# Gate steps, layer norm by blocks and rate rows in the prologue of an S4-convolution and SwiGLU training step

## The chip, the cores and the metric

One Trainium2 chip, one of its cores. The metric is the device time of one execution in microseconds (us). The kernel computes a forward pass and all gradients, in one launch.

## The reference, cut to what matters

```python
xn = layernorm(x)                          # x: 2048 x 576, bf16
# A: a diagonal state-space model as a long convolution, 128 states per channel
P = exp((dt * (A_re + 1j*A_im))[:, :, None] * l)     # 576 x 128 x 2048
K = einsum("dn,dnl,dn->dl", C, P, dt * B).real       # the kernel, 576 x 2048
s = irfft(rfft(xn padded) * rfft(K padded)) + xn * Dskip
# B: SwiGLU, 576 -> 4608 -> 576
h = silu(xn @ w1) * (xn @ w3)
g = silu(h @ w2)
out = x + s * g
# and the gradients of all inputs for a given grad_out
```

## The kernel before, in words

The program is written with a tile framework: each engine runs its own queue of instructions in order, and the framework places instructions by a priority (`pre(us)` and `at(us)`, lines 148 and 176, set it; they read like due times) and by orders written out by hand. `Chain` (line 77) ties every operation of one engine to the one before it; `in_order` (line 647) does the same for TensorE's matmuls of the prologue. A buffer of a pool is reused only when its readers are done.

The part that the change touches ends where the last gate step ends, about a third into the program.

*Prologue* (`prologue`, line 314). It loads the rates `A_re`, `A_im` and x (even 128-row tiles straight, odd ones turned round by a copy through DRAM, `odd_A_u`). A few matmuls against an identity (line 357) run while nothing else is ready for TensorE. From the step sizes dt it makes rho = A_re * dt, split into three bf16 parts `pc` (`split3`). `place_rates` (line 652) moves the parts of rho by small matmuls with the 0/1 matrix `place` into the layout `LR_` that the exponentials read, in five calls that cover the 36 chunks of 16 channels. `early_exps` (line 666) then makes 45 tiles of exponentials of 128 x 1024: matmuls of `LR_` with a selector give the exponents in PSUM (pool `ex_ps`, two buffers), ACT takes the exponential into one of four buffers `E_k`, SyncE stores it to `E_dram`. For the first 31 tiles every matmul is issued twice. Between them VectorE does the layer norm: `ln_stats` for the even and the odd tiles, `ln_root` once for all sixteen, `ln_scale`, and `ln_turn`, which transposes xn in ten pieces into `xnT`; `ln_fold` makes the sums and differences for the convolution. POOL makes the splits of the angles and the products `Wr`, `Wi`. Behind the last exponential (`exps_last`) ACT loads the silu table; `early_spectrum` computes the spectra of xn.

*Gate steps* (`ffn_hidden`, line 1064). 72 steps: nine blocks of 512 hidden columns by eight pairs of row tiles. A step has two halves (q = 0, 1); a half has eight matmuls of 512 columns and two of half depth into the PSUM tiles `pg` and `pu` (pool `f_ps`, two buffers each). ACT takes silu of pg into `s_t` and copies pu to `u_t`; pg is copied to `g_t` by VectorE or ACT; VectorE multiplies `h_t` = s_t * u_t. `h_t` is stored by SyncE, `g_t` and `u_t` by POOL (three buffers each). All silus wait for `exps_last`. The function is a generator: `prologue` steps it once, and the loop at the end of the program runs it through. `gate_time`, `gate_mark` and `step_at` (lines 1045 to 1062) place the steps: the first `LEAD` = 5 beside the spectra, then 36 beside the chunks, one each, the rest beside the convolution.

*Kernel chunks* (`ssm_kernel`, line 730). 36 chunks of 16 channels: `kgen_chunk` loads the exponentials `E_l` (three buffers), makes cosines and sines from matmuls (ACT, `cs_k`), multiplies on VectorE (`p_k`, `q_k`, `t_k`, `v_k`), and stores `q_k` and `p_k`; `kgen_sum` sums over the states on TensorE (`kps`) two chunks later. Then `ssm_conv` does the convolution, and `ffn_output` and the backward pass follow.

The gate steps' place, before:

```python
def gate_time(self, n):
    if n < self.LEAD:
        return 4.3 * n
    i = n - self.LEAD
    return self.KG[0] + 2 + self.KG[1] * i if i < 36 else self.KG[0] + self.KG[1] * 36 + 2 + 5.75 * (i - 36)
```

Of the kernel before, what the change touches and what calls it, by code (L numbers as in the profile page):

```python
# [14 lines left out]
FP32 = mybir.dt.float32  # L15
# [86 lines left out]
class K:  # L102
    LEAD, KG, GE = 5, (20, 6.0), (0, 8, 17, 26, 36)
# [48 lines left out]
    def setup_consts(self):  # L152
# [6 lines left out]
        self.pre(9)  # L159
# [45 lines left out]
    def ln_stats(self, tiles, small, last=None):  # L205
        half = self.cfg.D // 2
        for i in tiles:
            stats = small.tile([P, 2, 6], FP32, name="stats")
            self.V.bn_stats(stats[:, 0, :], self.xs[i][:, 0:half])
            self.V.bn_stats(stats[:, 1, :], self.xs[i][:, half:])  # L210
            if last is not None:
                self.V.bn_aggr(self.mv[:, last[0], :], last[1][:])
            last = i, stats
        return last

    def ln_root(self, small, last):
        self.V.bn_aggr(self.mv[:, last[0], :], last[1][:])
        self.root(small, self.rstd[:], self.mv[:, :, 1], self.cfg.LT)
        self.V.scalar_tensor_tensor(out=self.negmr[:], in0=self.mv[:, :, 0], scalar=-1.0, in1=self.rstd[:],
                                    op0=ALU.mult, op1=ALU.mult)  # L220
# [19 lines left out]
    def ln_turn(self, tiles, ps):  # L240
        nc, cfg = self.nc, self.cfg
        nfull, rem = cfg.D // P, cfg.D % P
        nt = len(tiles)
        xT = self.xnT.rearrange("p c (t q) -> p c t q", q=P)[:, :, tiles[0]:tiles[-1] + 1:2]
        for c in range(nfull + 1):
            pt = ps.tile([P, nt * P], FP32, name="t_ps")
            pv = pt[:].bitcast(BF16)[:, 0:nt * P] if c < nfull else pt[:]
            for j, i in enumerate(tiles):
                if c < nfull:
                    self.in_order(lambda: nc.tensor.transpose(pv[:, j * P:(j + 1) * P], self.xn_bf[:, i, c * P:(c + 1) * P],  # L250
                                                              self.ident_bf[:]))
                else:
                    for r in (0, rem):
                        self.in_order(lambda: nc.tensor.matmul(pv[r:r + rem, j * P:(j + 1) * P], lhsT=self.xn_bf[:, i, c * P:cfg.D],
                                                               rhs=self.ident_bf[:], start=True, stop=True))
            self.V.tensor_copy(out=xT[:, c], in_=pv.rearrange("p (t q) -> p t q", q=P))
            yield

    def ln_fold(self):
        for b in range(self.cfg.LT // 4):  # L260
            lo, hi = self.xn_bf[:, 4 * b:4 * b + 2, :], self.xn_bf[:, 4 * b + 3:4 * b + 1:-1, :]
            for k, op in enumerate((ALU.add, ALU.subtract)):
                self.V.tensor_tensor(out=self.xts[b][:, 2 * k:2 * k + 2, :], in0=lo, in1=hi, op=op)
                yield
# [49 lines left out]
    def prologue(self, matp, selp, xp, gate):  # L314
# [13 lines left out]
        with pool(name="par_tmp", bufs=1) as tmp, pool(name="par_pc", bufs=1) as pcp, pool(name="sel_tmp", bufs=1) as st, \  # L328
                pool(name="ln_sb", bufs=1) as lsb, pool(name="ln_small", bufs=4) as small, pool(name="dftgen", bufs=1) as dg, \
                pool(name="ex_l", bufs=1) as lp, pool(name="ex_e", bufs=4) as ep, pool(name="ex_u", bufs=1) as up, \  # L330
                pool(name="ex_ps", bufs=2, space=PS) as eps, pool(name="t_ps", bufs=2, space=PS, side="right") as tps:
# [3 lines left out]
            self.negmr = lsb.tile([P, LT], FP32, name="negmr")  # L335
            self.pre(0)
            even, odd = [*range(0, LT, 2)], [*range(1, LT, 2)]
# [10 lines left out]
            self.G.prev = self.odd_copy  # L348
            self.ln_load_odd(self.G)
            self.pre(0.5)  # L350
            self.selector_values(st, selp)
# [4 lines left out]
            for k in range(12):  # L356
# [10 lines left out]
            pd = tps.tile([P, 2 * 512], FP32, name="t_ps")  # L367
            nc.tensor.transpose(pd[:].bitcast(BF16)[:, 0:DT], lr[:], self.ident_bf[0:DT, 0:DT])
            self.S.activation(out=self.dt_col[:], in_=pd[:].bitcast(BF16)[:, 0:DT], func=ACT.Exp)
            self.dft_angles()  # L370
            self.S.activation(out=self.negmr[:, 0:1], in_=self.halfpi_col[:], func=ACT.Sin)
# [6 lines left out]
            pc = self.split3(self.V, tmp, rho)  # L378
            self.selector_base()
            LR_ = lp.tile([P, D // 16, N], BF16, name="lhs_r")  # L380
            self.place_rates(0, 4, pc, place, LR_, tps)
            self.place_rates(4, 12, pc, place, LR_, tps)
            ex = self.early_exps(LR_, ep, eps)
            run = lambda n: [next(ex) for _ in range(n - len(self.exps))]
# [3 lines left out]
            self.pre(9)  # L388
            self.V.scalar_tensor_tensor(out=thp[:], in0=self.A_im[:], scalar=1.0 / (2 * PI), in1=dt_b,
                                           op0=ALU.mult, op1=ALU.mult)  # L390
            for r, x, m in ((thr, thp, MAGIC), (r128, thr, MAGIC / 128)):
                self.V.tensor_scalar(out=t[:], in0=x[:], scalar1=m, scalar2=-m, op0=ALU.add, op1=ALU.add)
                self.V.tensor_tensor(out=r[:], in0=x[:], in1=t[:], op=ALU.subtract)
            for q, x in enumerate((thr, r128)):
                self.store3(q, self.split3(self.G, tmp, x))
            last = self.ln_stats(even, small)
            run(8)
            self.pre(9)
            self.load_rates(tmp, (1, 3, 5, 7))
            self.place_rates(12, 20, pc, place, LR_, tps)  # L400
            run(15)
            self.pre(17)
            last = self.ln_stats(odd, small, last)
            self.place_rates(20, 28, pc, place, LR_, tps)
# [1829 lines left out]
```

## Time and profile before

| | |
|---|---|
| median of 3 runs | 1754.08 us (1753.82 to 1766.34) |
| profiled execution | 1755.24 us, span 1753.1 us |
| TensorE, matmul | 1625.1 us busy, 93% of the span |
| VectorE | 1402.1 us, 80% |
| ACT (ScalarE) | 916.1 us, 52% |
| POOL (GpSimd) | 422.0 us, 24% |
| DMA | mean 225 GB/s |

Times in the profile are counted from the span's start. PE is TensorE's matmuls, PEld its weight loads, DVE is VectorE, SP is SyncE; a letter q behind an engine's name marks its queue, where DMAs are issued. A row of a timeline gives the start, the duration, engine, line, operation, what is written and read, and in brackets how long the engine had idled before and what ended that. Neighbouring alike instructions are merged (x4). A row by stretches gives for each engine its busy time and count, then the granted TensorE clock (1.00 is full), the DMA's busy share and its GB/s.

### The profile page before, as it was taken

Reading aid. Unit: us, or ns where it says so; the run is one execution under the profiler, and the core shown is the slowest. Engines: PE = TensorE matmul, PEld = TensorE weight load, DVE = VectorE, ACT = ScalarE, POOL = GpSimd, SP = SyncE. Lnnn points to the kernel's source line nnn. Section 1 sums busy time; section 2 is a strip of 40 time slices with the busy share of each in tenths; the row PEclk is TensorE's granted clock in tenths of the full one; section 3 lists DMA queues with packets and bytes.
Section 4 is the critical chain, followed back from the end, with each engine's and each line's share of the span. In section 5 each row is a group of like instructions: output and inputs, shape, how many; then the busy total and the mean of one; then the engine's idle time right before and its main releaser. Section 6 shows DMA issues by size and latency. Waiting matters only on the chain. (4 is left out here: it accounts for less than half of the span.)

```text
span 1753.1 us, 33144 instructions
## 1 busy us (share of the span) xinstructions
PE 1625.1 (93%) x12786; PEld 981.8 (56%) x12841; DVE 1402.1 (80%) x2170; ACT 916.1 (52%) x1674; POOL 422.0 (24%) x639
## 2 busy tenths in 40 slices
PE   7798788999997899889999999999999998999998
PEld 4453333444443677646555655555455566777766
DVE  6657798989894565587995899679799966899897
ACT  5667678777773111565866767565655501111111
POOL 7142121222223211111111212112121352122143
PEclk8899999999998999999999999999999999999999
DMA  6568897998778989848495776769899999999992
GB/s 204 208 210 288 287 314 257 322 340 259 254 264 208 232 208 191 225 144 235 146 278 161 206 205 202 196 172 268 196 262 225 251 222 240 227 205 216 231 201 51
DMA packets 624363, 394.86 MB, mean 225 GB/s; under 512 B 426798, under 2 KB 565678, under 8 KB 624206
## 3 DMA queue, kind: packets, MB, share of 16 engines
q1 hardware_dynamic: 565324, 264.49, 61.5%
q0 software_dynamic: 37088, 109.31, 19.8%
q10 hardware_dynamic: 21794, 18.95, 3.5%
q8 instruction: 100, 1.64, 0.4%
q14 instruction: 57, 0.47, 0.1%
HBM read 122.18 MB, written 182.13 MB: 174 GB/s over the span
## 5 line engine op out<-in xcount | busy, mean ns | idle before, releaser
L2017 PEld LDWEIGHTS <-acts 128*128 128x128 bf16 x2304 | 223.6, 98 | 63.9 <-issue 3.3
L1965 PE MATMUL pgw<-ggu,xn_bf 128*128 128x512 bf16 x1152 | 254.0, 379 | 0.1
L1122 PEld LDWEIGHTS <-xnT 128*128 128x128 bf16 x1152 | 107.8, 98 | 156.1 <-issue 53.5
L1500 DVE TENSOR_TENSOR pr_q<-et_ps,pz 128x1024 f32<-128x1024 f32 x144 | 176.0, 1223 | 21.1 <-PE et_ps L1494 11.9
L1965 PEld LDWEIGHTS <-xn_bf 128*128 128x128 bf16 x1152 | 111.5, 98 | 131.0 <-issue 0.4
L1504 DVE TENSOR_REDUCE S_b<-pr_q 128x64 f32<-128x1024 f32 x144 | 175.4, 1218 | 3.9
L1877 PE MATMUL ph<-w2T,goT 128*128 128x512 bf16 (+3 forms) x800 | 159.5, 368 | 10.6 <-DVE e L1237 3.7
L1122 PE MATMUL pg<-wmB_w,xnT 128*128 128x512 bf16 x539 | 151.5, 383 | 15.7 <-DVE g_t L1141 11.2
L1122 PE MATMUL pu<-wmB_w,xnT 128*128 128x512 bf16 x558 | 151.3, 383 | 1.7 <-issue 0.8
L1943 PE MATMUL pgw<-go_o,h_n 128*128 128x288 bf16 x1152 | 149.7, 287 | 1.1 <-ACT gh L1895 0.8
L1943 PEld LDWEIGHTS <-h_n 128*128 128x128 bf16 x1152 | 111.1, 98 | 31.2 <-issue 1.0
L1137 ACT ACTIVATE s_t<-pg 128x512 bf16<-128x512 f32 x144 | 87.2, 606 | 75.4 <-PE pu L1131 60.1
L2017 PE MATMUL px<-wT_ggu,acts 128*128 128x288 bf16 x896 | 123.5, 291 | 2.5 <-DMA wT_ggu<-in_B_w_dram 2.5
L1877 PEld LDWEIGHTS <-goT 128*128 128x128 bf16 (+1 forms) x800 | 65.0, 99 | 96.2 <-issue 41.1
L1151 POOL DMA_DIRECT2D G_dram<-g_t x72 | 52.3, 727 | 258.8 <-DVE g_t L1141 135.3
L1485 ACT COPY gz<-gz 64x1024 bf16<-64x1024 bf16 x36 | 37.6, 1043 | 147.1 <-DMA gz<-gK_dram 88.2
L2017 PE MATMUL px<-wA,acts 128*128 128x288 bf16 x832 | 109.8, 286 | 0.5 <-ACT gw13t L1980 0.5
L1971 POOL DMA_DIRECT2D out_dram<-gw x72 | 51.9, 722 | 207.6 <-ACT gw L1967 181.0
L778 ACT ACTIVATE cs_k<-et_ps 128x512 bf16<-128x512 int16 x180 | 93.2, 618 | 14.2 <-PE et_ps L776 11.5
L1948 POOL DMA_DIRECT2D out_dram<-gw x36 | 20.0, 555 | 330.6 <-ACT gw L1947 324.0
L1142 ACT CAST u_t<-pu 128x512 bf16<-128x512 f32 x144 | 86.4, 600 | 11.7 <-PE pu L1122 9.6
L1837 DVE TENSOR_TENSOR ggu<-ggu,h_n 128x1024 bf16<-128x1024 bf16 x72 | 48.9, 686 | 44.6 <-ACT ggu L1849 44.5
(341 smaller groups left out, 3190.4 us busy)
## 6 DMA issues: line engine op xcount, KB each, us to landing
G_dram<-g_t POOLq DMA_DIRECT2D x72, 256.0 KB, 4.5
U_dram<-u_t POOLq DMA_DIRECT2D x72, 256.0 KB, 4.7
H_dram<-h_t SPq DMA_DIRECT2D x72, 256.0 KB
Q_dram<-q_k SPq DMA_DIRECT2D x36, 512.0 KB
ggu<-G_dram POOLq DMA_DIRECT2D x18, 1024.0 KB, 8.1
h_n<-U_dram POOLq DMA_DIRECT2D x18, 1024.0 KB, 8.8
GG_dram<-ggu SPq DMA_DIRECT2D x36, 512.0 KB
GU_dram<-ggu SPq DMA_DIRECT2D x36, 512.0 KB
```

The source lines that it names most:

```text
L778: self.sin_last = nc.scalar.activation(out=CS[:, :, o:o + 256], in_=pt[:].bitcast(I16)[:, :, 0::2], func=ACT.Sin, scale=6.283184 / 2 ** 16)
L1122: ins = nc.tensor.matmul(pt[:], lhsT=xnT[:, c, ts], rhs=wm[w][:, c, :], start=(q == 0 and c == 0), stop=(q == 1 and c == nfull - 1))
L1137: nc.scalar.activation(out=s_t[:, :, q, :], in_=pgv, func=ACT.Silu)
L1142: nc.scalar.copy(out=u_t[:, :, q, :], in_=puv)
L1151: self.u_stores[step] = nc.gpsimd.dma_start(out=dst[fb * ng:(fb + 1) * ng, i0 // 4, :, i0 % 4:i0 % 4 + NT, :].rearrange("g p t f -> p g (t ...
L1500: nc.vector.tensor_tensor(out=pr[:], in0=T[z][:].rearrange("p s k d f j -> p (s k) (d f j)")[:, None] .to_broadcast([P, 2, 4, 4 * AV]), in ...
L1504: nc.vector.tensor_reduce(out=self.sums_of[-1][:, :, :, z, :, dg, d0:d0 + 8].rearrange("p r s k d -> p (r s) k d"), in_=pr[:].rearrange("p ...
L1877: prev = nc.tensor.matmul(dst(j, k), lhsT=lw, rhs=rh, start=start, stop=stop)
L1943: self.pe_last = nc.tensor.matmul(pgw[pi_][:, 0:pw], lhsT=hn[:, tt, fl * P:(fl + 1) * P], rhs=self.go_o[:, tt, po:po + pw], start=(tt == 0 ...
L1965: self.pe_last = nc.tensor.matmul(pw_[:], lhsT=self.xn_bf[:, tt, c * P:(c + 1) * P], rhs=ggu[:, :, tt, :], start=(n == 0), stop=(n == LT - 1))
L1971: self.gp(lambda: nc.gpsimd.dma_start(out=aps[names[w]][(c - 1) * P:(c + 1) * P, fb:fb + FG].rearrange("(c p) f -> p c f", p=P), in_=gw[:, ...
L2017: self.pe_last = nc.tensor.matmul(px[pi_][:, 0:pw], lhsT=acts[i][:, ai, fi, :], rhs=w[:, po:po + pw], start=(n == 0), stop=(n == len(steps ...
```

## The change

Twelve of the 72 gate steps move into the prologue, between batches of exponentials. They go in halves: `half()` runs one half of a step, `run(n)` makes n tiles of exponentials, `stats` takes statistics of single tiles. These halves are in the ordered chains of TensorE, ACT and VectorE. Batches of 7, 6, 9, 9 and 14 exponentials alternate with 4, 6, 6 and 8 halves. Exponentials are no longer multiplied twice, and have six buffers. The layer norm is done for blocks of four tiles: statistics, root, scale and transposition of a block follow each other. Only the rates of chunks 0 to 11 are placed by matmuls; the rest go from `pc` to DRAM and from there into `LR_`. The PSUM pool `f_ps` is opened ahead of the prologue and also serves placement and transposition; the spectra use `ex_ps`. Four more steps stay beside the spectra, then 24 steps run beside the 36 chunks, two for three, every other one with one of its g_t copies on ACT, and 32 beside the convolution. The chunks' loads of `E_l` go to POOL's queue, and the weights of gate blocks are loaded by a function of their own, one block ahead.

```diff
-    LEAD, KG, GE = 5, (20, 6.0), (0, 8, 17, 26, 36)
+    EARLY, LEAD, KG, GE = 12, 16, (20, 5.1), (0, 8, 17, 26, 36)
...
+    def ln_root(self, small, b):
+        sl = slice(4 * b, 4 * b + 4)
+        self.root(small, self.rstd[:, sl], self.mv[:, sl, 1], 4)
...
+            pd = self.front_ps()
+            self.in_order(lambda: nc.tensor.transpose(pd[:].bitcast(BF16)[:, 0:DT], lr[:], self.ident_bf[0:DT, 0:DT]))
...
+            self.rate_rows(pc, LR_)
...
+            self.place_rates(0, 4, pc, place, LR_, self.V.tensor_copy)
+            self.place_rates(4, 8, pc, place, LR_, self.S.copy)
+            stats(0, 2)
+            run(2)
+            self.place_rates(8, 12, pc, place, LR_, self.V.tensor_copy)
+            stats(1, 3)
+            run(3)
+            self.ln_root(small, 0)
+            self.ln_scale(range(0, 4))
+            self.ln_turn(0)
+            run(2)
+            self.pre(9)
+            self.load_rates(tmp, (1, 2, 3, 4))
+            half()
+            stats(4)
+            half()
+            stats(5, 6)
+            half()
+            stats(7)
+            half()
+            self.ln_root(small, 1)
+            run(3)
+            self.ln_scale(range(4, 8))
+            run(1)
...
+            self.ln_turn(1)
...
+            run(2)
...
+            half()
+            stats(8)
+            half()
+            stats(9, 10)
+            half()
+            stats(11)
+            half()
+            self.ln_root(small, 2)
+            self.ln_scale(range(8, 12))
+            self.ln_turn(2)
+            half()
+            stats(12)
+            half()
+            stats(13)
+            run(4)
+            stats(14, 15)
+            run(2)
+            self.ln_root(small, 3)
+            self.ln_scale(range(12, 16))
+            run(2)
+            self.ln_turn(3)
+            run(1)
+            for k in range(6):
+                half()
+                if k % 2:
+                    next(fold)
+            run(9)
+            for k in range(8):
+                half()
+                if k % 2:
+                    next(fold)
+            run(14)
...
+    def rate_rows(self, pc, LR_):
+        PR = self.dram.tile([3, D, N], BF16, name="PR_dram")
+        for k in range(3):
+            self.sy.dma_start(out=PR[k, 0:nfull * P].rearrange("(c p) n -> p c n", p=P), in_=pc[:, k, 0:nfull])
...
+                self.G.dma_start(out=LR_[r0:r0 + 8, 12:], in_=PR[k, H * h + 96:H * h + H, :].rearrange("(c e) n -> e c n", e=8))
...
-                E = ep.tile([P, 1024], BF16, name="E_k")
+                home, tag = (dg, ("dft_q", "dft_fr")[n % 6 - 4]) if n % 6 > 3 else (ep, "E_k")
+                E = home.tile([P, 1024], BF16, name="E_k", tag=tag)
-                for k in (0, 0, 1, 1) if n < 31 else (0, 1):
+                for k in range(2):
...
-                el = self.kg_load = nc.sync.dma_start(out=E[:], in_=self.E_dram[ch // 4, :, ch % 4 * TW:(ch % 4 + 1) * TW])
+                nc.gpsimd.dma_start(out=E[:], in_=self.E_dram[ch // 4, :, ch % 4 * TW:(ch % 4 + 1) * TW])
...
-        return self.KG[0] + 2 + self.KG[1] * i if i < 36 else self.KG[0] + self.KG[1] * 36 + 2 + 5.75 * (i - 36)
+        return self.KG[0] + 2 + 1.5 * self.KG[1] * i if i < 24 else self.KG[0] + self.KG[1] * 36 + 2 + 5.75 * (i - 24)
...
+        if n < self.EARLY:
+            self.pre(10 + 4 * n)
...
-                    if step >= self.LEAD + 36 or (q == 0 and step < self.LEAD):
-                        nc.scalar.copy(out=g_t[:, :, q, :], in_=pgv)
+                    if step >= self.LEAD + 24 or (not early and q == 0 and (step < self.LEAD or step % 2)):
+                        S.copy(out=g_t[:, :, q, :], in_=pgv)
```

237 lines of the change are left out of this document (119 added, 118 removed).

## The prediction

> **What bounds the kernel now.** I read busy time by stretch first, then each engine's timeline in the stretches that the change touches, then the waits of one queue. The change rearranges only the stages up to the end of the gate steps; behind them the built order of every engine is that of before, up to small swaps. So the sum is made of three stages: A, from the start to the first matmul of the first kernel chunk; B, the 36 chunks; C, the convolution with the rest of the gate steps.
>
> Stage B, by stretches (PE, PEld, DVE, ACT, POOL busy, granted clock, DMA share, GB/s):
>
> ```profile
> 132.00:200.00 68.00, 60.98 (x503) 26.12 (x508) 56.83 (x91) 53.86 (x106) 15.34 (x22) 0.97 0.88 308
> 200.00:228.00 28.00, 17.90 (x188) 7.90 (x193) 16.19 (x26) 12.44 (x26) 3.50 (x5) 0.82 0.66 220
> 228.00:300.00 72.00, 65.60 (x589) 28.93 (x598) 61.57 (x101) 60.78 (x121) 16.39 (x22) 1.00 0.86 282
> 300.00:376.00 76.00, 70.43 (x705) 32.34 (x715) 74.08 (x117) 59.34 (x118) 18.11 (x25) 1.00 1.01 341
> ```
>
> In the last row TensorE, VectorE and the DMA are full together (70.4 and 74.1 of 76, share 1.01). What one chunk and one gate step cost there, TensorE first (start, duration):
>
> ```profile
> 131.58 0.81 PE L776 MATMUL et_ps<-SEL,lhs_t 128*128 128x512 bf16 x3
> 132.22 1.03 PE L1122 MATMUL pg<-wmB_w,xnT 128*128 128x512 bf16 x4
> 379.44 0.68 PE L818 MATMUL kps<-v_k,q_k 128*64 128x32 bf16 x32
> 382.00 0.41 PE L917 MATMUL et_ps<-KT,dK 128*128 128x288 bf16 x2
> 413.88 1.04 PE L1122 MATMUL pg<-wmB_w,xnT 128*128 128x512 bf16 x4
> 417.98 1.04 PE L1122 MATMUL pg<-wmB_w,xnT 128*128 128x512 bf16 x4
> ...
> 300.87 0.41 DVE L785 TENSOR_TENSOR p_k<-cs_k,E_l 128x512 bf16<-128x512 bf16 x1
> 304.75 0.68 DVE L1141 CAST g_t<-pg 128x512 bf16<-128x512 f32 x1
> 305.35 0.68 DVE L1145 TENSOR_TENSOR h_t<-s_t,u_t 128x1024 bf16<-128x1024 bf16 x1
> 312.18 0.42 DVE L785 TENSOR_TENSOR p_k<-cs_k,E_l 128x512 bf16<-128x512 bf16 x1
> ```
>
> A gate step is 417.98 - 413.88 = 4.10 us of TensorE, a half 2.05. A chunk is 5 x 0.64/3 + 0.68 = 1.75. VectorE's p_k returns two chunks and two steps later: (312.18 - 300.87)/2 = 5.66 each, of which the step's three operations (two g_t, one h_t, 0.60 apart) are 1.81, the chunk 3.85.
>
> By the built order, the steps lie: before 0 ahead of the last exponential's matmul, 5.0 from there to the first chunk, 37.1 in B, 29.9 behind; after 13.2, 3.1, 25.1, 30.5.
>
> **Stage B.** It starts at 131.58 and ends when the first convolution matmul runs, at 382.00: 250.4 us. TensorE's work is 36 x 1.75 + 37.1 x 4.10 = 215, so 35 are something else, and one wait is most of it:
>
> ```profile
> 218.01 0.43 DVE L785 TENSOR_TENSOR p_k<-cs_k,E_l 128x512 bf16<-128x512 bf16 x1 [10.33 <-DMA E_l<-E_dram]
> SPq L755 <- DMA odd_grad_out<-in_grad_out_dram: 8.8, 1, 8.8
> ```
>
> SyncE's load of E_l waited for an unrelated large copy. With the restart behind it that is 14 us (10.3 of wait, 3.6 of half clock, below). The change puts E_l on POOL's queue, where it stands about three chunks ahead of its use, so this wait goes; what then waits for that copy is a store of q_k, which has four buffers. 21 us remain, in short waits of many kinds.
>
> After: 25.1 steps, every other one with a g_t copy on ACT, so 2.5 x 0.60 = 1.51 per step on VectorE: 3.85 + 0.70 x 1.51 = 4.90 a chunk. TensorE has 1.75 + 0.70 x 4.10 = 4.61. VectorE alone would need 36 x 4.90 = 176. The DMA is as near: by the four rows the stage moved 68 x 308 + 28 x 220 + 72 x 282 + 76 x 341 = 73 MB; a step's three stores
>
> ```profile
> G_dram<-g_t POOLq DMA_DIRECT2D x72, 256.0 KB, 4.5
> ```
>
> (G, U and H alike) and its eighth of a block of w1 and w3 (2 x 576 x 512 values, 1.18 MB) are 0.93 MB, so 12 steps fewer leave 62, and at the 341 GB/s of the full row these take 182. I take 182 and 18 of the 21 short waits, 200: **-50**. Bounds: -60 if the short waits halve, -42 if a wait nearly as long as the old one comes back on POOL's queue: there each E_l stands behind a G and a U store, which wait for VectorE's g_t and ACT's u_t, and behind E_l stand the next stores, for which only the third gate step after them waits (three buffers each).
>
> **Stage A.** The opening and the exponentials before:
>
> ```profile
> 3.18 0.16 PE L368 MATMUL t_ps<-ident_bf,lr 5*128 5x5 bf16 x1 [3.18 <-DVE place L87]
> 4.30 4.92 PE L357 MATMUL e_ps<-sel_dl,ident_bf 128*128 128x512 bf16 x12 [0.96 <-POOL sel_dl L553]
> 29.50 3.85 PE L661 MATMUL t_ps<-pc,place 128*32 128x128 bf16 x48
> 84.85 1.89 PE L683 MATMUL e_ps<-sel_val,lhs_r 80*128 80x512 bf16 x5
> ...
> 10.61 0.49 DVE L87 CAST pc<-sr_r 128x640 bf16<-128x640 f32 x1
> ...
> 18.10 1.94 ACT L87 ACTIVATE E_k<-e_ps 128x1024 bf16<-128x1024 f32 x2 [6.46 <-PE e_ps L683]
> ```
>
> *Opening.* The transposition that makes dt now stands in the ordered chain behind the 12 warm-up matmuls: it runs at 9.22 instead of 3.18, and ACT's chain, VectorE's phases and pc follow 6.0 later: 17.1. The 48 placements for chunks 0 to 7, at this row's 3.85, end at 21.0; then ACT copies (0.6, as u_t below) and loads its table (1.28), which before lay in idle time. First exponential 22.9 against 18.1. The earlier selector iota, the odd rows' loads and the zeroed lhs_r lie in this time; alone they would have saved 3.
>
> *Work in turns.* The exponentials are ACT's, the halves TensorE's:
>
> ```profile
> 68.14 8.46 ACT L87 ACTIVATE E_k<-e_ps 128x1024 bf16<-128x1024 f32 x9 [0.25 <-ACT E_k L87]
> 87.80 0.74 ACT L87 ACTIVATE rho<-rho 128x640 f32<-128x640 f32 x1
> 88.54 1.28 ACT L87 ACT_TABLE_LOAD   x1
> 89.83 0.20 ACT L87 ACTIVATE junk<-halfpi_col 128x1 f32<-128x1 f32 x1
> 139.36 0.62 ACT L1142 CAST u_t<-pu 128x512 bf16<-128x512 f32 x1
> 139.82 0.66 ACT L1137 ACTIVATE s_t<-pg 128x512 bf16<-128x512 f32 x1
> ```
>
> 45 x 0.94 = 42.3 and 24 x 2.05 = 49.2 follow each other, because both engines keep their order and PSUM holds two exponentials and two halves ahead: 22.9 + 42.3 + 49.2 = 114.4. Each of four changes from halves to exponentials costs the last silu and copy (1.1) and a table load (1.28), 2.4; each change back saves 1.4, since the last exponential's matmul runs 1.4 before its activation ends. 114.4 + 9.6 - 5.6 = 118.4.
>
> The Trainium skill, page "ScalarE: Activation LUTs", section "Table sets: the hidden batching unit", advises against such turns: do all calls of one table set together. Its section "What ACT_TABLE_LOAD costs" gives 1283 ns and a drain of 1380 ns; with that drain four times the sum would be 5.5 higher, an estimate. The load agrees, the drain doesn't show: the load starts where rho ends, 88.54, and junk where the load ends.
>
> *Waits for the layer norm.* Each block of four tiles is a chain on VectorE and then TensorE:
>
> ```profile
> 35.37 0.76 DVE L87 BATCH_NORM_STATS2 stats<-xt 128x6 f32<-128x288 bf16 x2
> 36.16 0.76 DVE L87 BATCH_NORM_STATS2 stats<-xt 128x6 f32<-128x288 bf16 x2
> 44.66 1.13 DVE L87 TENSOR_SCALAR rt_v<-mv 128x16 f32<-128x16 f32 x1
> 51.95 0.18 DVE L87 SCALAR_TENSOR_TENSOR rt_a<-rstd 128x16 f32<-128x16 f32 x1
> 52.16 0.17 DVE L87 TENSOR_TENSOR rt_a<-rt_a,rt_v 128x16 f32<-128x16 f32 x1
> 52.86 5.52 DVE L87 TENSOR_SCALAR xn_bf<-xt,rstd,negmr 128x576 bf16<-128x576 bf16 x16
> ...
> 82.01 1.06 PE L250 MATMUL t_ps<-ident_bf,xn_bf 128*128 128x128 bf16 x8
> ```
>
> Statistics 0.79 a tile; root 13 x 0.21 = 2.7, or 8.2 (44.66 to 52.86) while POOL computes; scale 5.52/4 = 1.4; 24 transpositions 3.2, last copy 0.7. Block 0: on TensorE the first two exponentials take 21.0 to 23.1 at half clock, the third placement (24 matmuls, 1.9) follows to 25.0, and its copy (0.7, as g_t's) to 25.7. Only behind that copy do tiles 1 and 3 come: 25.7 + 1.6 + 2.7 + 1.4 + 3.2 gives 34.6, and then the next exponential's matmul and activation, 36; the three before it are done at 29: 7. Block 1: copies and product (1.9), root, scale, turn, 8 to 9, against 2.4 + 4 x 0.94: 2. Block 2 stands between halves with nothing beside it: 2.2 + 2.7 + 1.4 + 3.2 + 0.7 = 10. Block 3: its root falls on POOL's Wr and Wi, 1.8 + 2.4 + 8.2 + 1.4 + 3.2 = 17, less the 9.9 of 8 exponentials: 6. Together 25; bounds 7 (block 0's alone) and 36 (two more roots beside POOL).
>
> *Clock.* The repeated exponential matmuls that filled TensorE are gone.
>
> ```profile
> 20.00:24.00 4.00, 4.00 (x13) 1.80 (x12) 3.93 (x10) 2.08 (x3) 3.56 (x3) 0.50 0.68 231
> 88.00:92.00 4.00, 3.78 (x14) 1.48 (x14) 2.45 (x6) 3.98 (x7) 0.00 (x0) 0.67 0.32 118
> 220.00:225.00 5.00, 2.85 (x7) 0.99 (x7) 4.93 (x10) 1.09 (x2) 0.72 (x1) 0.50 0.55 150
> 225.00:230.00 5.00, 4.84 (x49) 1.99 (x49) 3.55 (x6) 2.75 (x6) 0.00 (x0) 0.78 1.03 383
> ```
>
> Gate matmuls restarting at 88.45 lost 4 x 0.33 = 1.3; the restart at 220 lost 2.5 + 1.1 = 3.6. I take 1.5 at three restarts, 4.5; 18 is the upper end (five at 3.6).
>
> 118.4 + 25 + 4.5 = 147.9, last exponential matmul 146.5. From there to the first chunk it was 131.58 - 86.74 = 44.8; 1.9 steps fewer take off 7.8, and the spectra, now in the exponentials' PSUM, wait 1.4 for the last of them: 38.4. First chunk at 184.9: **+53**.
>
> At nothing: the rate rows through DRAM (144 of 216 placement matmuls less on TensorE and three copies on VectorE; the four stores and six loads have some 25 us before exponential 15 needs them; late, they cost their lateness) and two more E_k buffers, whose cover is the turns themselves: stores land while the halves run, and only the last 14 exponentials run through. The 12 early steps also issue 24 stores on POOL and 12 on SyncE. Behind POOL's stand the splits of the angles and Wr, Wi, which nothing needs before the last turn is over; behind SyncE's, which wait for h_t, stand stores of exponentials, with six buffers to wait. The gate weights of the first block are now loaded ahead of pc's stores on SyncE, in the opening's first 10 us, beside the odd rows; tiles 1 and 3 aren't read before 25.7.
>
> **Stage C.** 0.6 step more: **+2** (0 if TensorE's waits for hc at the end take it).
>
> Sum: 53 - 50 + 2 = +5 on the profiled execution's 1755.24 (its span 1753.1 and 2.1 around it), which lies 1.2 above the median of the three runs, 1754.08: 1759.
>
> **Rivals.** *The waits go* (faster): VectorE gets each block done under the exponentials ahead, and B sheds half of its short waits; 18 and some 9 less: 1759 - 27 = 1732. For it: with ACT's exponentials running, VectorE has nothing but the block to do. Against: block 2's place.
> *The clock stays down* (slower): the row at 20 us has TensorE busy 4.00 of 4.00 and still at 0.50, which went on for 12 us. If each run of halves begins with 9 us at half, four lose 4.5 and the short one 4.1, 22 instead of 4.5: 1776. With 7 us it is 3.5 five times, 1772, where slower begins. The Trainium skill, page "TensorE: Matmul & The Clock Gate", section "What's actually happening", says some 3.4 us of sustained work restore the clock; this row speaks against it.
> *E_l's new queue stalls* (the change doesn't remove the wait, only moves it): 14 back, 1773.
>
> **How the numbers follow.** Forecast 0.50 (1748 to 1770: the 25 us of block waits between 15 and 36, B within -56 to -46), waits go 0.19, clock 0.19, queue 0.12. About 1%, 17.5 us, is what a measurement of this kernel can tell from no change; faster begins below 1736.5, slower above 1771.6. Faster takes 0.14, most of it from the first rival; slower 0.15 of the clock's 0.19, 0.08 of the queue's and 0.05 of the forecast's tail. The range leaves out the outer half of the two far rivals: 1737 to 1782.
>
> **What would show it.** First exponential near 23; eight more table loads; TensorE idle 8 to 10 us ahead of the fifth gate step; first chunk at 185; chunks 5.0 apart and no 10 us wait for E_l; half clock only briefly in the gate runs. Wrong if A ends outside 170 to 200 or B takes other than 190 to 208. The sum also rests on the stages behind the gate steps being moved and not changed; a different time there would be an error of its own.

## The result, and the profile after

Over 20 runs each, the changed kernel took 1767.8 us in the median and the kernel before 1755.9; the ratio is 1.0067, interval 1.0040 to 1.0095. The interval leaves out 1, so the changed kernel is slower, by two thirds of a per cent; that is inside the 1% that the prediction counts as no change. The profiled executions of after (1782.11 us) and of b_el_pr below are among the slow ones of their kernels in the later stages, so their times behind the output products are not used; up to the first of these after agrees with its repetition, a_again, within 1 us.

The three stages, in the view of single lines for TensorE (count, shortest/middle/longest, first and last start). Before, after, and after profiled once more:

```profile
L776 PE MATMUL et_ps<-SEL,lhs_t x180: 376/379/634, 131.6 to 373.0; 128*128 128x512 bf16 x180
L917 PE MATMUL et_ps<-KT,dK x128: 282/286/297, 382.0 to 492.8; 128*128 128x288 bf16 x128
L1225 PE MATMUL po<-w2a,hcA x192: 286/286/286, 545.9 to 711.7; 128*128 128x288 bf16 x192
```

```profile
L826 PE MATMUL et_ps<-SEL,lhs_t x180: 376/379/634, 187.6 to 378.2; 128*128 128x512 bf16 x180
L967 PE MATMUL et_ps<-KT,dK x128: 282/286/448, 385.7 to 494.9; 128*128 128x288 bf16 x128
L1301 PE MATMUL po<-w2a,hcA x192: 285/286/287, 551.1 to 717.8; 128*128 128x288 bf16 x192
```

```profile
L826 PE MATMUL et_ps<-SEL,lhs_t x180: 376/379/634, 187.8 to 378.5; 128*128 128x512 bf16 x180
L967 PE MATMUL et_ps<-KT,dK x128: 282/286/297, 386.0 to 494.0; 128*128 128x288 bf16 x128
L1301 PE MATMUL po<-w2a,hcA x192: 286/286/286, 550.2 to 711.3; 128*128 128x288 bf16 x192
```

The first line gives the start of the chunks, the second their end, the third the first output product.

| us | before | after | difference | predicted |
|---|---|---|---|---|
| A, to the first chunk | 131.6 | 187.6 | +56.0 | +53 |
| B, the chunks | 250.4 | 198.1 | -52.3 | -50 |
| C, to the first output product | 163.9 | 165.4 | +1.5 | +2 |
| sum | 545.9 | 551.1 | +5.2 | +5 |

From the first output product to the end: 1753.1 - 545.9 = 1207.2 before, and 1758.5 - 550.2 = 1208.3 in a_again. Behind that point TensorE runs the same matmuls in the same order in the three profiles, but for the gate steps: 14 matmuls of theirs lie behind it before, 32 in after and in a_again, and 34 in a_dt_first below, in whose trace no record of a gate matmul is missing. So this cut leaves one gate step, 4.1 us of TensorE, more behind it in the changed kernel, and the +1.5 of stage C is too good by that. Behind the last gate matmul TensorE goes on with the same product; before, after and a_again:

```profile
569.97 3.10 PE L1225 MATMUL po<-w2g,hcA 128*128 128x288 bf16 x24
576.04 3.10 PE L1301 MATMUL po<-w2g,hcA 128*128 128x288 bf16 x24
567.25 3.10 PE L1301 MATMUL po<-w2g,hcA 128*128 128x288 bf16 x24
```

There after is 6.1 us behind and a_again 2.7 us ahead. Between the two points TensorE waits for loads of `hcB` from DRAM: 8.6 us before, 7.3 in after, 2.1 in a_again.

The chunks of after, by stretches (PE, PEld, DVE, ACT, POOL busy, granted clock, DMA share, GB/s):

```profile
187.60:250.00 62.40, 56.35 (x544) 24.97 (x548) 56.72 (x91) 53.96 (x109) 17.58 (x27) 0.97 0.92 325
250.00:274.00 24.00, 17.72 (x198) 8.12 (x198) 18.84 (x29) 19.07 (x40) 5.37 (x9) 0.98 0.86 287
274.00:300.00 26.00, 23.74 (x270) 11.15 (x274) 23.53 (x44) 19.07 (x40) 9.38 (x14) 0.88 1.01 333
300.00:385.70 85.70, 76.71 (x809) 34.75 (x817) 81.42 (x128) 76.55 (x155) 22.98 (x35) 1.00 1.00 327
```

In the last row VectorE is busy for 81.4 of 85.7 us and the DMA all the time. Summed over the rows the stage moved 64 MB. The dip in the second row is the copy of grad_out again. SyncE's queue waits 10.6 us for it, at a load of `lhs_t`, and the store of p_k stands behind that load. From the waits of SyncE's queue and from the timeline:

```profile
SPq L776 <- DMA odd_grad_out<-in_grad_out_dram: 10.6, 1, 10.6
267.52 0.43 DVE L835 TENSOR_TENSOR p_k<-cs_k,E_l 128x512 bf16<-128x512 bf16 x1 [4.87 <-DMA PZ_dram<-p_k]
274.79 0.59 PE L1184 MATMUL pg<-wmB_w,xnT 128*128 128x512 bf16 x1 [5.58 <-DVE g_t L1212]
```

The prologue of after, from its timelines:

```profile
8.28 0.17 PE L370 MATMUL pf<-ident_bf,lr 5*128 5x5 bf16 x1
16.22 1.87 PE L698 MATMUL pf<-pc,place 128*32 128x128 bf16 x46 [1.16 <-DVE pc L87]
20.02 1.94 ACT L87 ACTIVATE E_k<-e_ps 128x1024 bf16<-128x1024 f32 x2
...
31.15 1.94 ACT L87 ACTIVATE E_k<-e_ps 128x1024 bf16<-128x1024 f32 x2 [5.67 <-PE e_ps L733]
...
61.25 0.59 ACT L87 CAST u_t<-pu 128x512 bf16<-128x512 f32 x1 [0.27 <-PE pu L1184]
65.97 1.25 DVE L87 SCALAR_TENSOR_TENSOR rstd<-rt_a,rstd 128x4 f32<-128x4 f32 x1
67.45 3.31 DVE L87 TENSOR_SCALAR xn_bf<-xt,rstd,negmr 128x576 bf16<-128x576 bf16 x4
68.22 0.29 PE L245 MATMUL pf<-ident_bf,xn_bf 128*128 128x128 bf16 x1 [7.00 <-DVE xn_bf L87]
73.28 1.49 PE L1184 MATMUL pg<-wmB_w,xnT 128*128 128x512 bf16 x3 [0.33 <-DVE xnT L87]
85.49 1.94 ACT L87 ACTIVATE E_k<-e_ps 128x1024 bf16<-128x1024 f32 x2 [0.23 <-PE e_ps L733]
87.66 1.02 ACT L87 ACTIVATE E_k<-e_ps 128x1024 bf16<-128x1024 f32 x1 [0.23 <-PE e_ps L733]
92.59 1.02 ACT L87 ACTIVATE E_k<-e_ps 128x1024 bf16<-128x1024 f32 x1 [3.91 <-PE e_ps L733]
151.49 0.73 ACT L87 ACTIVATE rho<-rho 128x640 f32<-128x640 f32 x1
```

The first exponential starts at 20.0. The fifth gate step starts at 73.3; the last gate matmul ahead of it had ended at 61.2, so the gate steps stood still for 12 us, in which TensorE had only the block's transpositions to do. The two rows on VectorE in that gap are slow: one step of the root, 0.16 elsewhere, takes 1.25, and the scaling 3.31 instead of 1.45. Exponentials come in pairs 2.17 apart. They end at 151.5. How a run of halves begins, by stretches, here the second run:

```profile
51.11:54.60 3.49, 3.27 (x8) 1.06 (x7) 2.12 (x3) 2.66 (x3) 3.01 (x3) 0.50 0.58 173
54.60:61.20 6.60, 6.60 (x33) 2.43 (x32) 5.36 (x14) 3.92 (x7) 6.25 (x9) 0.99 0.77 258
```

Halves begin anew five times (31.8, 51.1, 73.3, 92.3 and 117.1). In the first 2.5 to 3.5 us the granted clock was 0.59, 0.50, 0.61, 0.51 and 0.58, then 0.99 to 1.00.

### The profile page after: what moved, and what is told of

It reads as the page before. It is cut to its first block, busy times and chain, and to the rows that moved or that the text cites. A ratio compares the mean times of both kernels' runs of the same rounds, so it can differ in the third digit from the quotient of the medians.

```text
span 1780.3 us, 32835 instructions
## 1 busy us (share of the span) xinstructions
PE 1622.2 (91%) x12572; PEld 971.4 (55%) x12623; DVE 1401.1 (79%) x2196; ACT 930.5 (52%) x1696; POOL 441.3 (25%) x681
## 5 line engine op out<-in xcount | busy, mean ns | idle before, releaser
L1184 PE MATMUL pg<-wmB_w,xnT 128*128 128x512 bf16 x545 | 159.7, 392 | 12.0 <-DVE g_t L1212 8.0
L1184 PE MATMUL pu<-wmB_w,xnT 128*128 128x512 bf16 x556 | 156.8, 390 | 1.6 <-issue 0.9
L1208 ACT ACTIVATE s_t<-pg 128x512 bf16<-128x512 f32 x120 | 74.4, 620 | 57.1 <-PE pu L1197 49.4
L2043 ACT CAST gw<-pgw 128x512 bf16<-128x512 f32 x72 | 42.0, 583 | 71.6 <-PE pgw L2041 64.2
```

The source lines that it names most:

```text
L1184: go = lambda: nc.tensor.matmul(pt[:], lhsT=xnT[:, c, ts], rhs=wm[w][:, c, :], start=(q == 0 and c == 0), stop=(q == 1 and c == nfull - 1))
L1208: S.activation(out=s_t[:, :, q, :], in_=pgv, func=ACT.Silu)
```

## The experiments

Times are of one profiled execution unless runs are named. "First chunk" is the first chunk's first matmul, 131.6 before and 187.6 to 187.8 after. Five variants have that one execution alone: a_el_sync 1799.5 us, a_dt_first 1761.2, a_no_silu 1783.0, a_exps_double 1781.7, a_ln_thr 1767.2. What they show is read from the stages and not from these times.

### a_again: the changed kernel once more

> The changed kernel itself, profiled a second time. Theory 1 (the first 550 us are settled by the order of the instructions, the rest of the loss is scatter in the later stages, whose instruction order is the same in both kernels on every engine): first chunk matmul at 187.6 and first convolution matmul at 385.7, each within 1 us of the first profile, first output product within 1 us of 551.1; from there to the end about 1207 us as in the kernel before (545.9 to 1753.1), so a span near 1758. Theory 2 (the change costs time in the later stages too, through where its data lies or which queue its transfers use): the first 550 us the same, but 1215 us or more from the first output product to the end.

187.8, 386.0 and 550.2, then 1208.3 to the end; the run took 1760.39 us. By its numbers this is theory 1: the first 550 us repeat, and at the first output product 4.3 us are lost. But the execution makes this loss up again: its last matmul on Z starts at 1153.0, against 1154.6 before, and its whole loss lies behind that.

### b_el_pool and a_el_sync: the queue of E_l, alone and left out

In b_el_pool, on the kernel before (a_el_sync is the reverse on the changed kernel):

```diff
-                el = self.kg_load = nc.sync.dma_start(out=E[:], in_=self.E_dram[...])
+                nc.gpsimd.dma_start(out=E[:], in_=self.E_dram[...])
...
-                    self.conv_loads(el, ...)
+                    self.conv_loads(self.kg_load, ...)
```

`kg_load` is the store of q_k there.

> The kernel before with one part of the change alone: the loads of E_l go out on GpSimd's queue instead of SyncE's, and the transfers that were ordered behind a load of E_l are ordered behind the store of Q. Nothing else differs. Theory of the prediction (the 10.3 us wait for E_l and the half clock behind it go with the queue): first chunk matmul stays at 131.6, the chunk stage falls from 250.4 by 10 to 14 us, to 236 to 240, and no wait of VectorE for E_l over 2 us is left; total 10 to 14 us below the kernel before. Rival (the copy of grad_out then holds another transfer of SyncE's queue, the store of p_k, as the profile of the changed kernel shows a 4.9 us wait for it): the chunk stage falls by only 4 to 8 us and VectorE waits about 5 us for p_k's buffer.

> The changed kernel with the loads of E_l back on SyncE's queue, the rest of the change kept. Theory of the prediction: the wait of 10 us for E_l comes back in the chunk stage, with its clock restart, and the stage goes from 198 to 208 to 212 us; the opening stays at 187.6. Rival (the shorter chunk stage comes from the gate steps taken out of it alone): the stage stays within 4 us of 198.

First chunk and first convolution matmul of b_el_pool, then of a_el_sync, and from the waits of a_el_sync VectorE's for E_l (us in all, times, longest):

```profile
L776 PE MATMUL et_ps<-SEL,lhs_t x180: 376/379/586, 132.9 to 359.9; 128*128 128x512 bf16 x180
L917 PE MATMUL et_ps<-KT,dK x128: 282/286/297, 368.9 to 479.1; 128*128 128x288 bf16 x128
```

```profile
L826 PE MATMUL et_ps<-SEL,lhs_t x180: 376/379/634, 187.2 to 399.5; 128*128 128x512 bf16 x180
L967 PE MATMUL et_ps<-KT,dK x128: 282/286/297, 408.1 to 514.7; 128*128 128x288 bf16 x128
```

```profile
DVE p_k L835 <- DMA E_l<-E_dram: 13.8, 1, 13.8
```

| chunk stage, us | E_l on SyncE | E_l on GpSimd | queue |
|---|---|---|---|
| 37 gate steps in it | 250.4 | 236.0 | -14.4 |
| 25 gate steps in it | 220.9 | 198.1 | -22.8 |
| 12 steps fewer | -29.5 | -37.9 | |

In the kernel before, the queue alone is worth 14.4 us, as the prediction priced it. SyncE's queue still waits for the copy of grad_out, 12.0 us, but no load of E_l stands behind it any more. The kernel takes 1744.8 us in the median of 7 runs, ratio to before 0.9918 (0.9886 to 0.9950): this one part of the change alone is faster than both kernels, though than the one before by less than 1%. In the changed kernel the queue matters more than expected (22.8; the wait was 13.8 there), and the twelve steps taken out give back 37.9 of the 49.2 us of TensorE that they need.

### a_dt_first: the transposition of dt ahead of the warm-up matmuls

```diff
             self.exps, self.e_stores, self.fixed = [], [], None
+            pd = self.front_ps()
+            self.in_order(lambda: nc.tensor.transpose(pd..., lr[:], ...))
             for k in range(12):
```

> The changed kernel with the transposition of the log of dt ahead of the twelve warm-up matmuls, as in the kernel before. Theory of the prediction (the time of the first exponential moves everything behind it): pc is ready about 5 us sooner, the first exponential starts near 15 to 16 us instead of 20.0, and the first chunk matmul comes 4 to 5 us earlier, at 183. Rival (layer-norm block 0 sets the first gate half, and it waits for the odd tiles of the input, not for the exponentials): the first exponential is earlier, but the first gate half stays within 1.5 us of 31.8 and the first chunk matmul within 1.5 us of 187.7.

```profile
11.17 1.05 PE L698 MATMUL pf<-pc,place 128*32 128x128 bf16 x46 [1.17 <-DVE pc L87]
28.18 1.70 PE L1184 MATMUL pg<-wmB_w,xnT 128*128 128x512 bf16 x4
```

The first exponential starts at 14.4, 5.6 sooner. The first gate half comes at 28.2 instead of 31.8: block 0 keeps 2 of the 5.6. First chunk 185.0, 2.7 sooner. So neither: half of the gain is passed on. 3.6 us had come through at the first half; the largest loss behind it is block 3, for which ACT waits 9.2 us where after has 3.9: VectorE's root of that block starts sooner here, runs beside more of GpSimd's products and takes 9.7 us (75.99 to 85.67) where after takes 4.2.

### a_no_silu: no table loads between the batches

```diff
-                        S.activation(out=s_t[:, :, q, :], in_=pgv, func=ACT.Silu)
+                        S.activation(out=s_t[:, :, q, :], in_=pgv, func=ACT.Copy if early else ACT.Silu)
```

> The changed kernel with Copy in the place of Silu in the twelve early gate steps (their silu is left out), so that ScalarE keeps the table of Exp through all batches; the instructions' count and sizes stay, the table loads at the turns go. Theory of the prediction (of each pair of turns only the 1.28 us load from halves to exponentials is on the path, the other lies beside TensorE's first half): eight loads fewer, the exponentials after each run of halves start 1.3 us sooner, the first chunk matmul 4 to 6 us earlier, at 182 to 184. Rival A (both loads of a pair are on the path): 9 to 11 us earlier, 177 to 179. Rival B (the turns are set by TensorE's half clock and by the layer norm): within 2 us of 187.7.

The kernel leaves out the silu of the early steps. First chunk 188.2: rival B. The loads go and the exponentials behind a run of halves start sooner, at 41.28 instead of 43.30 behind the first run, but what comes next is a block of the layer norm, and it comes no sooner. ACT at block 3, and one step of VectorE's root for it:

```profile
81.06 4.39 DVE L87 TENSOR_SCALAR rstd<-rt_a 128x4 int32<-128x4 int32 x1
94.32 1.02 ACT L87 ACTIVATE E_k<-e_ps 128x1024 bf16<-128x1024 f32 x1 [12.12 <-PE e_ps L733]
```

The wait is 12.1 where after has 3.9. The exponentials ahead of it start at 74.1 instead of 80.2, but the root of block 3 then takes 10.9 us (78.65 to 89.58) instead of 4.2, because GpSimd's products run beside it. So the loads' time was gained and lost again in the layer norm; what they would be worth without GpSimd beside the root was not run. The advice to batch one table's calls (the Trainium skill, page "ScalarE: Activation LUTs", section "Table sets: the hidden batching unit", which the prediction weighed) would have gained nothing in this kernel as it stands.

### a_exps_double: the matmuls of the first 31 exponentials issued twice again

```diff
-                for k in range(2):
+                for k in (0, 0, 1, 1) if n < 31 else (0, 1):
```

> The changed kernel with each matmul of the first 31 exponentials issued twice, as the kernel before did, so that TensorE stays busy between them. Theory of the prediction (TensorE idles under the exponentials, its clock falls, and the next run of halves starts at half clock; three restarts of 1.5 us): the granted clock in the exponentials' stretches rises, the exponentials run at 0.94 instead of 1.09 us a piece and the first halves of a run at full clock; first chunk matmul 4 to 6 us earlier, 182 to 184. Rival (the doubled matmuls run at half clock anyway, as at 20 to 32 us of the kernel before, and then cost more than an exponential): the exponentials take 1.2 us or more a piece and the first chunk matmul is later than 190.

First chunk 204.1: the rival. Stretches on TensorE (columns as above), and one exponential from ACT's timeline:

```profile
20.00:32.00 12.00, 11.36 (x62) 5.34 (x61) 7.79 (x30) 6.31 (x6) 3.79 (x6) 0.50 0.83 187
32.00:40.00 8.00, 8.00 (x33) 3.24 (x32) 1.64 (x3) 3.33 (x3) 0.00 (x0) 0.50 0.32 109
```

```profile
96.61 1.02 ACT L87 ACTIVATE E_k<-e_ps 128x1024 bf16<-128x1024 f32 x1 [0.68 <-PE e_ps L733]
```

TensorE is busy for 8.00 of 8.00 us and its clock stays at 0.50. The exponentials then take 1.71 each. Keeping TensorE busy with repeats bought no clock in these stretches and cost 16 us; why the clock stays down is not shown. The Trainium skill, page "TensorE: Matmul & The Clock Gate", section "What's actually happening", gives about 3.4 us of sustained work until the clock is full; this row does not agree.

### a_ln_early, a_ln_pool, a_ln_thr: the layer norm

```diff
             self.ln_turn(0)
+            stats(8, 9, 10, 11)
...
+            self.ln_root(small, 2)
+            self.ln_scale(range(8, 12))
             half()
-            stats(8)
+            stats(12)
...
             half()
+            self.ln_root(small, 3)
+            self.ln_scale(range(12, 16))
             run(4)
```

The statistics of tiles 13 to 15 follow between the next halves, and block 2's root and scaling are gone from their old place.

> The changed kernel with the layer norm's VectorE work pulled forward: statistics of tiles 8 to 11 right behind the first block's transposes, root and scaling of block 2 ahead of the third run of gate halves, statistics of tiles 12 to 15 within that run, root and scaling of block 3 right behind the sixth step. The counts of all instructions stay. Theory of the prediction (the waits of the layer norm are on the path and nothing covers them): TensorE's gap of 12.3 us ahead of the fifth gate step shrinks to about 3 us, the 3.9 us wait at block 3 goes, first chunk matmul at 176 to 179 instead of 187.6, total 8 to 11 us below the changed kernel, so 1757 to 1760 if that is at 1768. Rival (VectorE then delays the gate halves, or the exponentials wait instead): first chunk matmul later than 183.

First chunk 190.0: the theory's time is missed, the gap before the fifth step is 1.1 us but 4.3 are lost on g_t earlier, and block 3 is worse. The median of 4 runs is 1778.3 us, ratio to before 1.0107 (1.0036 to 1.0178). VectorE's root of block 3 with GpSimd beside it:

```profile
82.87 4.41 DVE L87 TENSOR_TENSOR rt_a<-rt_a,rt_v 128x4 f32<-128x4 f32 x1
83.30 1.27 POOL L87 TENSOR_TENSOR Wr<-Wr,dt_col 128x640 f32<-128x640 f32 x1
84.51 1.40 POOL L87 TENSOR_TENSOR Wi<-C_re_bf,B_im_bf 128x640 f32<-128x640 bf16 x1
85.86 1.39 POOL L87 TENSOR_TENSOR t<-C_im_bf,B_re_bf 128x640 f32<-128x640 bf16 x1
```

One operation on 128x4 values, 0.16 us otherwise, ends when three of GpSimd's have passed; the whole root took 14.9 us (75.54 to 90.43). So the next runs moved GpSimd's work behind the last block. a_ln_pool moved GpSimd's lines only:

> The layer norm pulled forward as in a_ln_early, and GpSimd's own arithmetic (the splits of the two phases with their stores, and the products for Wr and Wi) moved behind the transposes of the last layer-norm block, so that no root runs beside it. Theory (GpSimd's 128x640 operations hold up VectorE's instructions: the thirteen of the root took 2.6 us alone and 14.8 us beside them in a_ln_early): both later roots are back at 2.6 to 3 us, the wait of the third run of gate halves for g_t (4.3 us) goes, the gap ahead of the fifth gate step is 3 to 4 us, first chunk matmul at 176 to 179. Rival (the order on VectorE alone delayed the halves, GpSimd has nothing to do with it): the root of block 2 still takes over 5 us and the first chunk matmul stays behind 185. Second rival (the moved arithmetic delays what needs it: the rows of phases for the first chunk, the stores of g_t and u_t behind it on GpSimd's queue): the roots are short, but the first chunk matmul comes no earlier than 183.

First chunk 188.4, median 1762.6 us in 10 runs, ratio to before 1.0027 (0.9992 to 1.0061). Its edit did not do what it was for: GpSimd starts as soon as VectorE's phases are there, wherever its lines stand, so it ran beside the roots as before (the scaling of block 3 took 4.75). a_ln_thr moved VectorE's five steps that make the phases too:

> The layer norm pulled forward as in a_ln_early, and now VectorE's five steps that make the two phases stand behind the transposes of the last layer-norm block too. GpSimd's splits and products wait for these phases, so they can no longer run beside a root (in a_ln_pool they had stayed where they were, because nothing held them back: the roots of blocks 2 and 3 took 5.8 and 10.5 us there). Theory (GpSimd's 128x640 operations hold up VectorE's small instructions, and this is what the layer norm loses): roots of all four blocks at 2.5 to 3 us, no wait of the third run for g_t, gap ahead of the fifth gate step 3 to 4 us, first chunk matmul at 175 to 179 against 187.7. Rival (the roots are slow for another reason, or the work of GpSimd is late for the first chunk): roots over 4 us, or short roots and the first chunk matmul later than 183.

```profile
72.01 0.16 DVE L87 TENSOR_SCALAR rt_v<-mv 128x4 f32<-128x4 f32 x1
74.49 0.16 DVE L87 SCALAR_TENSOR_TENSOR negmr<-mv,rstd 128x4 f32<-128x4 f32 x1
74.69 1.45 DVE L87 TENSOR_SCALAR xn_bf<-xt,rstd,negmr 128x576 bf16<-128x576 bf16 x4
```

The two later roots take 2.5 and 2.6 us, first chunk 181.7. The mechanism is shown: a_ln_pool differs only in where VectorE's phases stand, and its roots took 5.7 and 10.5 us. It is worth 6.7 us of the first chunk against a_ln_pool and 6 against the changed kernel, not the 9 to 13 expected. The Trainium skill, page "SBUF — State Buffer", section "Who interferes with whom", says that certain VectorE operations and GpSimd lock each other out of shared ports for a whole instruction; the rows agree in kind, though 4.41 us is longer than any one of GpSimd's.

### a_ln_thr_dt: both

> a_ln_thr with the transposition of the log of dt first, as in a_dt_first. Theory: the two gains add, 2.7 us for the transposition (as a_dt_first measured on its own) on top of a_ln_thr, first chunk matmul at 172 to 176, chunk stage unchanged at 197 to 199, total 12 to 15 us below the changed kernel. Rival: the chunk stage takes the gain back, because its stores and loads bound it (over 203 us).

First chunk 176.1, chunk stage 374.3 - 176.1 = 198.2, median 1746.1 us in 4 runs, ratio to before 0.988 (0.9795 to 0.9964). More than the sum: 11.6 against 6.0 + 2.7. One reason is on record: in a_dt_first most of the sooner start was lost in the root of block 3, 9.7 us, and here this root takes 2.6. The changed kernel's idea can be made faster than the kernel before, by about what one line of it, E_l's queue, gives alone (1744.8 us); both have that line, so no run shows that the moved steps add to it.

### b_el_single: b_el_pool with single exponential matmuls

The edit is that of a_exps_double in reverse, in the kernel before.

> b_el_pool with each matmul of the exponentials issued once instead of twice for the first 31, as the changed kernel has it. Theory from a_exps_double (the doubled matmuls do not bring the clock back, and cost 1.71 us an exponential at half clock where single ones cost 1.09): the exponentials between 18 and 32 us run at 1.1 instead of 1.7 us, first chunk matmul 4 to 6 us earlier, at 127 to 129, chunk stage as in b_el_pool (236), total about 1740. Rival (in the kernel before the doubled matmuls do bring the full clock, at 32 us, and without them all 45 exponentials and the transposes beside them run at half clock): the granted clock from 32 to 80 us falls from near 1.0 to 0.6, and the first chunk matmul comes later than 133.

The stretches from 18 to 50 us of b_el_pool, then of b_el_single:

```profile
18.00:32.00 14.00, 14.00 (x47) 6.26 (x46) 10.40 (x29) 7.99 (x8) 9.78 (x10) 0.50 0.56 172
32.00:50.00 18.00, 16.70 (x149) 10.19 (x148) 13.05 (x32) 11.39 (x13) 16.96 (x16) 0.97 0.67 213
```

```profile
18.00:32.00 14.00, 12.57 (x73) 6.88 (x72) 12.39 (x34) 9.34 (x10) 9.63 (x10) 0.58 0.76 226
32.00:50.00 18.00, 14.54 (x84) 7.58 (x83) 14.53 (x33) 13.63 (x15) 16.89 (x16) 0.72 0.70 233
```

The rival is half right: with single matmuls the clock from 32 to 50 us is 0.72 instead of 0.97. But ACT does more in both stretches, and the first chunk comes at 125.4 against 132.9. Median 1737.8 us in 4 runs, ratio 0.9854 (0.9761 to 0.9946): the lowest median seen, but its interval overlaps those of b_el_pool, b_el_pr and a_ln_thr_dt.

### b_el_pr: the place of the tensors in DRAM

```diff
             pc = self.split3(self.V, tmp, rho)
+            PR = self.dram.tile([3, D, N], BF16, name="PR_dram")
+            for k in range(3):
+                self.sy.dma_start(out=PR[k, 0:nfull * P]..., in_=pc[:, k, 0:nfull])
+            self.sy.dma_start(out=PR[:, nfull * P:D]..., in_=pc[0:D - nfull * P, :, nfull])
```

> b_el_pool with the DRAM tensor PR that the changed kernel adds: allocated at the same place in the order of tensors (442 KB, so that every later tensor in DRAM lies that much further on) and stored once by the same four transfers; nothing reads it. The question is what lengthens the later stages, in which both kernels have the same order of instructions: from the first output product to the end the kernels built on the one before took 1203.1 to 1207.2 us, those built on the changed one 1205 to 1232 us. Theory L (where the tensors lie in DRAM): first output product within 2 us of 532.1, from there to the end 1212 us or more, total at 0.996 to 1.000 of the kernel before. Rival (the place has nothing to do with it; scatter, or something handed on from the first stages): 1202 to 1209 us from the first output product to the end, total at 0.989 to 0.995 as for b_el_pool.

First output product at 531.5; median 1741.0 us in 8 runs, ratio 0.9884 (0.9833 to 0.9934), just below the rival's 0.989 to 0.995 and far from theory L's 0.996 to 1.000. The profiled execution took 1228.8 us behind the product, as theory L had it, but it was the second longest of the eight. Five of them, 1735.8 to 1742.1 us, are like b_el_pool's seven (1737.3 to 1750.2); three took 1755.0 to 1762.9. So the place in DRAM doesn't lengthen the later stages as a rule; that it has a part in the three long runs is not ruled out.

## Why the prediction was right, and where it was not

**The sum.** +5 was forecast up to the end of these stages, +5.2 came at the first output product. That the two agree is in part luck: at this cut the changed kernel has one gate step more still to do, and behind the last gate matmul after stands at +6.1 and a_again at -2.7. The median difference is 11.9, so a good part of it, in a_again all, lies where the prediction had zero.

**Stage A** was +56.0 for +53, with errors that cancelled: 2.9 us less in the opening, 0.2 less in the waits, 6.7 more under clock, and 0.9 less from the last exponential to the first chunk. *Opening*: 20.0, not 22.9. The warm-up was done at 8.3, not 9.2, and the placements took 1.87, not 3.85: that row, taken from between exponentials, was the wrong neighbour. The granted clock was 0.50 for both (16.2 to 18.1 in after, 29.5 to 32.0 before); what makes the difference stays open. *Work in turns*: a gate step is 4.10 us, as said. *Waits for the layer norm*: 5.7, 3.1, 12.1 and 3.9 for the predicted 7, 2, 10 and 6, 24.8 for 25, but not for the stated reason, and so by luck. The prediction put GpSimd's hold on block 3 and gave block 2 a clean root of 2.7; in after, block 2's root (4.4) and scaling were held by GpSimd too, and block 3's root, 4.2, took half of the 8.2 feared. (Its own terms for block 3, 17 less 9.9, give 7 and not 6.) *Clock* is the term that was mis-sized: 20.0 + 42.3 + 49.2 + 9.6 - 5.6 + 24.8 = 140.3, and the exponentials end at 151.5, so 11.2 are left where 4.5 stood. This is a remainder, but most of it can be read. The five runs of halves took 9.4, 10.1, 4.9, 14.0 and 17.7 us for 4, 4, 2, 6 and 8 halves, 6.9 more than 24 x 2.05: the prediction had three restarts of 1.5, and there were five of 1.4. The rest was missed as a kind: with the clock down (0.66 from 80 to 100 us in a_again) a pair of exponentials takes 2.17 instead of 1.88, which needs no restart.

**Stage B**: 198.1 for 200. The stall was priced at 14 and b_el_pool measured 14.4 in the place it was predicted from. That a store of q_k would wait next was wrong: it was p_k's, 4.87 us. That VectorE and the DMA bound the rest fits the last stretch, and the 12 steps gave 37.9, not their 49.2.

**Stage C**: +1.5 for +2, at a cut that flatters it by 4.1 us. Up to the product behind the last gate matmul it is 190.3 in after and 181.3 in a_again for 188.0 before, +2.3 and -6.7: what TensorE waits for `hcB` scatters by more than the term. The prediction had named this wait, as a way to 0 and not below.

**The rivals.** *The waits go*: they did not by themselves; a_ln_thr_dt shows what it takes. *The clock stays down*: each run of halves began at half clock for about 3 us, not 9, and the rest of that cost sat in the exponentials. *E_l's new queue stalls*: no wait for E_l was left. The sum had four table loads on the path, 1.28 each; a_no_silu shows that the layer norm, held by GpSimd, takes up their time when they go, so these 5 us stand in the sum but could not be saved alone.

**The later stages** are the error that the prediction had named as one of its own. From the first output product to the end three kernels built on the one before took 1203.1, 1205.4 and 1207.2 us (without b_el_pr's 1228.8), the nine profiles built on the changed one 1205.1 to 1231.6, in the middle 1213.1; some 4 us of the difference are the gate matmuls that lie behind this point there. Nearly all of the rest lies behind the last matmul on Z, 1154.6 before: from there to the end 597.6 to 600.3 us in the first three, 599.0 to 623.6 in the nine, in the middle 610.4. The groups overlap. One wait grows with this time: TensorE's for ACT's copy of `gz`, which in turn waits mostly for the load of `gz` from DRAM. Before, and in a_ln_pool (611.8 us), behind the last matmul on Z:

```profile
PE et_ps L1494 <- ACT gz L1485: 4.9, 2, 3.2
PE et_ps L1569 <- ACT gz L1560: 20.5, 5, 15.2
```

It is 4.9 to 7.4 us in the three; of the nine it is 4.8 and 6.8 in the two shortest, 7.5 in a_again and 9.2 to 22.1 in the six longest. What delays these loads, and what the first stages hand on to them, stays open.

## What to carry to other kernels

Before moving work, look for one long wait and whose queue it stands in: here one load on another queue brought the first output product 13.8 us forward (532.1 for 545.9), and the rebuilt prologue without it set it 25.0 back (a_el_sync, 570.9). Work moved out of a stage is given back only down to what else bounds the stage; here the prologue with 12 more steps took 56 us longer, and the chunks gave back 38. Here a short chain on VectorE was only short when GpSimd computed nothing beside it, and to move GpSimd's work one had to move what it waits for. While that hold was there, it also ate what two other edits gained ahead of it (a_dt_first, a_no_silu): a gain of nothing says little about an edit until the next wait is known.

## What the runs showed of the hardware

A 128x4 operation on VectorE took up to 4.41 us in a_ln_early beside GpSimd's 128x640 operations, against 0.16 alone; thirteen of them took 14.9 against 2.6. TensorE stayed at half clock through 8.00 of 8.00 busy us in a_exps_double and 14.00 of 14.00 in b_el_pool; gate halves had the full clock after 2.5 to 3.5 us. A table load took 1.28 us each time, and taking eight of them away did not bring the first chunk forward (188.2 against 187.7), because the root behind them took longer.
